# Another list of batches: optional work placed elsewhere between the scores of an attention kernel

## The chip, the cores and the metric

The kernel runs on one core of a Trainium2 chip. The metric is the device time of one execution in microseconds; three runs of the kernel before gave 647.3, 646.79 and 646.97, median 646.97. The core's engines are TensorE (PE in the profile, with its weight loads as PEld), VectorE (DVE), ScalarE (ACT), GpSimd (POOL) and SyncE (SP), which here only issues transfers. All of them run their own instruction streams in order and wait for each other on semaphores.

## The reference, cut to what matters

Two independent results are computed from two inputs of 2048 rows by 448 columns and put side by side.

```python
q = heads(x @ wq)              # 16 heads of 28 columns
k = x @ wk; v = x @ wv         # one key and one value head, shared by all 16
p = softmax(q k^T * 28**-0.5)  # 16 x 2048 x 2048
a = concat(p v) @ wo

X = rfft2(x2); X = X * (w_r + 1j * w_i); b = irfft2(X)
```

The attention part dominates: 16 heads times 2048 queries times 2048 keys of exponentials. The spectral filter (a transform over columns and rows, a product, and the way back) is much smaller and is cut into pieces that are slipped in between.

## The kernel before

**Projections.** The first 69 us of the profile form queries, keys and values, and the first pieces of the filter's forward transform. The change leaves them alone, except for one piece that it moves (below, F).

**Steps.** What follows is 256 steps: 4 blocks of 512 queries, times 4 groups of 4 heads, times 16 blocks of 128 keys. A step has four scores, one for each head: a matmul (line 867, `s<-qa,ka`, 128 keys by 512 queries) that fills one PSUM bank. ScalarE makes the exponential of a bank into SBUF (line 811, `p<-s`), and then the bank is free again. The output phase multiplies the exponentials with the values (line 822, `s<-p,vs`; eight records for a step) and sums 16 steps into one bank. After the 16th step VectorE transposes that bank out (line 826) and a new group of 4 heads begins. The group needs its own query tile `qa`, made by `build_q`: three VectorE instructions (lines 217, 219, 208), eight small transfers (line 213) and, once those have landed, one transfer of 512 KB (line 215), all issued by SP. `build_q` is put into VectorE's list after the fourth step of the group before. In this document q4 and q5 are the query tiles of steps 64 and 80.

**Banks.** There are eight PSUM banks: six named `s`, and `sx` and `po`. One of them holds the output being summed. So seven are left for scores and for the optional units below; each is taken by `take()` and handed back by `give()`, which decide at build time, by a rough clock of their own, which bank is taken next.

**Batches.** The list PLAN has 50 strings; one string is one batch. Of each batch all scores are formed first, then the outputs. In a string `-` is a score whose exponential ScalarE makes from the bank; `k` is a score of the batch's last step that VectorE copies out of its bank (line 873, `k<-s`), so that ScalarE can make the exponentials of that step later, two wide instructions (line 890); `e` is a score of the last step whose exponential ScalarE writes at once. The last step's outputs are formed in the next batch. Since its four `k` scores stand among the first eight, a batch whose last step opens a new group needs that group's `qa` from its second score on. Batches of five steps have 20 scores ("fives"), batches of six have 24 ("sixes").

**Units.** The other letters are pieces of other work, each with its own bank:

- F, once: the last piece of the filter's first stage (line 159), read out by VectorE and stored for the second stage.
- A, 16 times (lines 556 to 558, three matmuls): second stage; VectorE then reads the bank three times (601 to 603) and goes on for five more instructions (609 to 611, 587, 588).
- B, 16 times (lines 556 to 558 too, with `g2`): the stage after; VectorE copies the bank out (625), and after every second B the tile is stored by SP (629).
- W, 48 times, in fours (line 731, 11 matmuls): the output projection of one block of 128 rows; one bank for four, read by VectorE (738).
- Z, 32 times, in twos: the last stage, in turn two transforms (line 655, read by line 658) and two more (line 669, read by lines 673 to 675). In the text z stands for a pair of the first kind and y for a pair of the second.

VectorE also normalises each finished group (lines 703, 708, 722, 723, 718), with 8 KB transfers behind it (line 692 on SP, 695 on GpSimd). VectorE, ScalarE and TensorE run in the order in which the program writes them. Between the letters the function `passed` lets waiting VectorE work go in by the rough clock; so another string also changes VectorE's order. The transfers of SP and GpSimd are ordered by the scheduler.

`spread(n, units, lazy, start, rest)` writes a string: it sets unit number j behind about 4(n-1)·(j+start)/(units+rest) scores. A larger start sets the units later; a smaller rest spreads them wider.

Of the kernel before, what the change touches and what calls it, by code (L numbers as in the profile page):

```python
# [37 lines left out]
def spread(n, units, lazy=4, start=0.9, rest=0.85):  # L38

    m = 4 * n - 4  # L40
    out = [(float(i), "-") for i in range(m)]
    out += [(j + 0.5 if j < lazy else m + 0.1 * j, "k" if j < lazy else "e") for j in range(4)]
    out += [(m * (j + start) / (len(units) + rest) - 0.4, u) for j, u in enumerate(units)]
    return "".join(k for _, k in sorted(out)).replace("X", "WWWW").replace("Y", "ZZ")


PLAN = ["eeeeF", "eeee"] + 4 * [spread(2, "", 0)]
FIVE, SIX = spread(5, "BA"), {u: spread(6, u) for u in ("X", "Y", "BAX", "XBB")}
PLAN += [spread(5, "A", 4, 1.6), spread(5, "A")] + 11 * [FIVE] + [SIX["X"], FIVE, SIX["X"], SIX["BAX"], FIVE]
PLAN += [SIX["XBB"], spread(5, "")]  # L50
PLAN += 4 * [SIX["Y"]] + 4 * [SIX["X"]] + 7 * [SIX["Y"]] + 4 * [SIX["X"]] + 3 * [SIX["Y"]] + 2 * [spread(5, "Y")]


WARM = 10, 10
# [3 lines left out]
def kernel(ctx: ExitStack, tc: tile.TileContext, t: dict):  # L58
# [713 lines left out]
    where, total = {}, 0  # L772
    for tokens in PLAN:
        n, x = sum(k in "-ke" for k in tokens) // 4, 0
# [71 lines left out]
    begin = 0  # L846
    for tokens in PLAN:
        n = sum(k in "-ke" for k in tokens) // 4
# [273 lines left out]
```

## Time and profile before

| | before |
|---|---|
| median of three runs | 646.97 us |
| the profiled execution | 646.39 us |
| its span, first to last instruction | 644.5 us |
| TensorE busy | 639.0 us |
| ScalarE busy | 552.6 us |
| VectorE busy | 370.6 us |
| mean granted TensorE clock | 0.999 |

The profiled execution lies 0.58 us under the median, and its time is 1.9 us more than its span. Matmuls overlap in the records, so TensorE looks busy even where the next matmul starts late; a wait shows in the distance between starts rather than as idle time. The view of stretches, asked for from one batch's first score to the next one's, gives a batch's length and each engine's busy time in it. In the timeline view equal instructions that follow each other are merged into one row with a count.

### The profile page before, as it was taken

Reading aid. Unit: us, or ns where it says so; the run is one execution under the profiler, and the core shown is the slowest. Engines: PE = TensorE matmul, PEld = TensorE weight load, DVE = VectorE, ACT = ScalarE, POOL = GpSimd, SP = SyncE. Lnnn points to the kernel's source line nnn. Section 1 sums busy time; section 2 is a strip of 40 time slices with the busy share of each in tenths; the row PEclk is TensorE's granted clock in tenths of the full one; section 3 lists DMA queues with packets and bytes.
Section 4 is the critical chain, followed back from the end, with each engine's and each line's share of the span. In section 5 each row is a group of like instructions: output and inputs, shape, how many; then the busy total and the mean of one; then the engine's idle time right before and its main releaser. Section 6 shows DMA issues by size and latency. Waiting matters only on the chain.

```text
span 644.5 us, 12021 instructions
## 1 busy us (share of the span) xinstructions
PE 639.0 (99%) x4470; PEld 381.5 (59%) x4470; DVE 370.6 (58%) x683; ACT 552.6 (86%) x1011; POOL 79.9 (12%) x150
## 2 busy tenths in 40 slices
PE   9999999999999999999999999999999999999997
PEld 7877555555555556655555566556655566556655
DVE  5999538989997937465543523354545342363531
ACT  5655999999998989988999898998999898998891
POOL 3022301001211110001020300011031100010110
PEclk9999999999999999999999999999999999999999
DMA  8766953446734522213242403014241403131001
GB/s 275 263 182 167 269 135 101 115 99 155 189 87 112 142 59 72 55 59 103 56 114 59 114 16 80 29 41 122 52 122 42 103 15 80 44 92 20 30 31 60
DMA packets 36113, 63.83 MB, mean 99 GB/s; under 512 B 7905, under 2 KB 23922, under 8 KB 35084
## 3 DMA queue, kind: packets, MB, share of 16 engines
q1 hardware_dynamic: 30832, 49.60, 27.7%
q0 software_dynamic: 4640, 12.48, 7.5%
q10 hardware_dynamic: 576, 0.92, 0.4%
q8 instruction: 36, 0.59, 0.4%
q14 instruction: 29, 0.24, 0.1%
HBM read 30.04 MB, written 14.75 MB: 69 GB/s over the span
## 4 chain that ended last, share of the span: by engine, by line
PE 96%; DMA 1%; DVE 1%; SPq 1%; issue 0%; ACT 0%; ACTq 0%; DVEq 0%
PE s L867 30%; PE s L822 23%; PE po L822 7%; PE s L342 6%; PE sx L867 5%; PE sx L822 4%; PE po L867 4%; PE s L731 4%; PE s L140 2%; PE s L655 2%; PE s L669 2%; PE po L731 1%; PE pbb L159 1%; DMA qa<-qa 1%; PE s L290 1%; PE s L558 1%
## 5 line engine op out<-in xcount | busy, mean ns | idle before, releaser
L811 ACT ACTIVATE p<-s 128x512 f32<-128x512 f32 x632 | 340.1, 627 | 37.1 <-PE s L867 31.4
L867 PE MATMUL s<-qa,ka 128*128 128x512 f32 x782 | 238.0, 407 | 0.3 <-DMA qa<-qa 0.2
L867 PEld LDWEIGHTS s<-qa,ka 128*128 128x128 f32 x782 | 143.2, 188 | 73.7 <-issue 33.1
L873 DVE COPY k<-s 128x512 f32<-128x512 f32 x131 | 84.1, 683 | 125.4 <-PE s L867 125.4
L822 PE MATMUL s<-p,vs 128*32 128x512 f32 x1112 | 132.3, 595 | 0.0
L890 ACT ACTIVATE k<-k 128x1024 f32<-128x1024 f32 x88 | 90.3, 1108 | 0.0
L822 PEld LDWEIGHTS s<-p,vs 128*32 128x32 f32 x1112 | 33.5, 109 | 72.6 <-issue 70.9
L811 ACT ACTIVATE p<-sx 128x512 f32<-128x512 f32 x109 | 68.3, 626 | 7.0 <-PE sx L867 6.4
L811 ACT ACTIVATE p<-po 128x512 f32<-128x512 f32 x83 | 52.8, 636 | 4.8 <-PE po L867 2.3
L867 PE MATMUL sx<-qa,ka 128*128 128x512 f32 x130 | 53.2, 409 | 0.0
L867 PE MATMUL po<-qa,ka 128*128 128x512 f32 x112 | 45.2, 403 | 0.0
L822 PE MATMUL s<-k,vs 128*32 128x512 f32 x296 | 38.7, 594 | 0.0
L822 PE MATMUL po<-p,vs 128*32 128x512 f32 x328 | 38.5, 594 | 0.0
L695 POOL DMA_DIRECT2D ol<-ol x36 | 18.0, 508 | 130.1 <-DVE ol L718 65.4
L679 POOL TENSOR_TENSOR yo<-y 128x226 f32<-128x226 f32 x16 | 9.5, 596 | 190.7 <-DVE y L675 98.1
L867 PEld LDWEIGHTS sx<-qa,ka 128*128 128x128 f32 x130 | 24.4, 188 | 12.7 <-issue 5.0
L873 DVE COPY k<-po 128x512 f32<-128x512 f32 x27 | 18.5, 683 | 16.4 <-PE po L867 16.2
L867 PEld LDWEIGHTS po<-qa,ka 128*128 128x128 f32 x112 | 21.1, 188 | 7.6 <-issue 2.5
L822 PE MATMUL sx<-p,vs 128*32 128x512 f32 x208 | 24.8, 595 | 0.0
L826 DVE STREAM_TRANSPOSE osb<-s 128x512 f32<-128x512 f32 x11 | 7.9, 716 | 29.2 <-PE s L822 29.2
L822 PEld LDWEIGHTS po<-p,vs 128*32 128x32 f32 x328 | 9.8, 110 | 21.9 <-issue 21.3
L342 PE MATMUL s<-xh,wqh 128*128 128x512 f32 x56 | 22.7, 404 | 0.0
(224 smaller groups left out, 780.6 us busy)
## 6 DMA issues: line engine op xcount, KB each, us to landing
qa<-qa SPq DMA_DIRECT2D x15, 512.0 KB
raw<-xa SPq DMA_DIRECT2D x16, 256.0 KB
xb<-xb SPq DMA_DIRECT2D x8, 512.0 KB
qa<-qh SPq DMA_DIRECT2D x64, 64.0 KB
qa<-ql SPq DMA_DIRECT2D x60, 64.0 KB
ob<-yo SPq DMA_DIRECT2D x16, 226.0 KB
t<-bs SPq DMA_DIRECT2D x16, 225.0 KB
wr<-wr POOLq DMA_DIRECT2D x16, 225.0 KB, 4.6
```

The source lines that it names most:

```text
L140: mm(pa[r0:r0 + 32, e, o0:o0 + n], f[:, 2 * r + k, 2 * p + e, h], cs1[:, 2 * r + k, :n], start=True, stop=True)
L342: mm(pq, w[:, j, gs], x[:, j], start=(j == 0 and n == 0), stop=(j == 3 and n == 1))
L655: mm(pz[:w, j], c2["c", q][:, j, o0:o0 + w], c2["F", q][:, j], start=True, stop=True)
L669: mm(py[:, k], z[:w, r, js], cs3[:w, k], start=True, stop=True)
L679: nc.gpsimd.tensor_tensor(yo[:, 0:2], y1[:, 0], y1[:, 1], op=ALU.add)
L695: nc.gpsimd.dma_start(ol[c][o, g].bitcast(F32), ol[c][r, 0].bitcast(F32))
L731: mm(p, x[c][:, g, s], w, start=(g == 0 and n == 0), stop=(g == NG - 1 and n == 2))
L811: nc.scalar.activation(tiles[-1][:, h % 2], sc, AF.Exp, scale=SCALE)
L822: mm(po[c, g][32 * i:32 * i + 32], vs[:, kc], ps[i // 2][:, i % 2], start=(n == 1), stop=(n == 16))
L867: begun.append(mm(sc, ka[:, kc * 128:(kc + 1) * 128], qa[c, g][:, h], start=True, stop=True))
L873: nc.vector.tensor_copy(keep[h // 2][:, h % 2], sc)
L890: nc.scalar.activation(p, p, AF.Exp, scale=SCALE)
```

## The change

Only PLAN changes. The numbers of batches (50), of fives and sixes, of scores of each kind and of units of each kind stay the same.

```diff
-PLAN = ["eeeeF", "eeee"] + 4 * [spread(2, "", 0)]
-FIVE, SIX = spread(5, "BA"), {u: spread(6, u) for u in ("X", "Y", "BAX", "XBB")}
-PLAN += [spread(5, "A", 4, 1.6), spread(5, "A")] + 11 * [FIVE] + [SIX["X"], FIVE, SIX["X"], SIX["BAX"], FIVE]
-PLAN += [SIX["XBB"], spread(5, "")]
-PLAN += 4 * [SIX["Y"]] + 4 * [SIX["X"]] + 7 * [SIX["Y"]] + 4 * [SIX["X"]] + 3 * [SIX["Y"]] + 2 * [spread(5, "Y")]
+PLAN = ["eeee"] + ["eeeeF"] + [spread(2, "", 0, 1.05)] + 3 * [spread(2, "", 0)] + [spread(5, "A", 4, 1.6)]
+PLAN += [spread(5, "BA", 4, 0.9, 0.6)] + [spread(5, "A")] + 6 * [spread(5, "BA", 4, 0.9, 0.6)]
+PLAN += [spread(5, "BA", 4, 0.75, 0.6)] + 3 * [spread(5, "BA", 4, 0.9, 0.6)] + 2 * [spread(6, "X")]
+PLAN += [spread(5, "BA", 4, 0.9, 0.6)] + [spread(6, "BAX")] + [spread(5, "BAB", 4, 0.9, 0.6)]
+PLAN += [spread(6, "BX")] + [spread(6, "Y")] + [spread(5, "")] + 2 * [spread(6, "Y")]
+PLAN += [spread(6, "Y", 4, 0.9, 0.6)] + [spread(6, "X")] + [spread(6, "X", 4, 0.9, 0.6)] + [spread(6, "X")]
+PLAN += [spread(6, "Y")] + [spread(6, "X", 4, 0.9, 0.6)] + 3 * [spread(6, "Y")]
+PLAN += [spread(6, "Y", 4, 0.9, 0.73)] + [spread(6, "Y")] + [spread(6, "Y", 4, 0.9, 0.73)]
+PLAN += 3 * [spread(6, "X")] + [spread(6, "Y")] + [spread(6, "X", 4, 0.9, 0.73)] + [spread(5, "Y")]
+PLAN += [spread(6, "Y")] + [spread(6, "Y", 4, 1.2)] + [spread(5, "Y")]
```

Written out, the batches whose string changes (counted from 0; the rest is the same):

```
batch   before                        after
0, 1    eeeeF / eeee                  eeee / eeeeF
7       -k-k-k-k----A--------         -k-k-k-k--B------A----
8       -k-k-k-k-B------A-----        -k-k-k-k----A--------
9-14    -k-k-k-k-B------A-----        -k-k-k-k--B------A----
15      -k-k-k-k-B------A-----        the same
16-18   -k-k-k-k-B------A-----        -k-k-k-k--B------A----
20      -k-k-k-k-B------A-----        -k-k-k-k------WWWW----------
21      -k-k-k-k------WWWW----------  -k-k-k-k--B------A----
23      -k-k-k-k-B------A-----        -k-k-k-kB-----A----B---
24      -k-k-k-k-WWWW-----B-----B-----  -k-k-k-k--B-------WWWW-------
25      -k-k-k-k------------          -k-k-k-k------ZZ----------
26      -k-k-k-k------ZZ----------    -k-k-k-k------------
29      -k-k-k-k------ZZ----------    -k-k-k-k-------ZZ---------
31      -k-k-k-k------WWWW----------  -k-k-k-k-------WWWW---------
33      -k-k-k-k------WWWW----------  -k-k-k-k------ZZ----------
34      -k-k-k-k------ZZ----------    -k-k-k-k-------WWWW---------
38, 40  -k-k-k-k------ZZ----------    -k-k-k-k-------ZZ---------
44      -k-k-k-k------WWWW----------  -k-k-k-k------ZZ----------
45      -k-k-k-k------ZZ----------    -k-k-k-k-------WWWW---------
46      -k-k-k-k------ZZ----------    -k-k-k-k----ZZ--------
48      -k-k-k-k----ZZ--------        -k-k-k-k---------ZZ-------
```

VectorE's and SP's orders follow. In batch 17, for one, the three instructions of `build_q` for q5 stood behind everything that follows A; after the change they stand right behind the three that read A's bank (603), ahead of 609 to 611, 587 and 588. In SP's list the 512 KB transfer of the query tile of step 32 comes behind a store of B's tile (629) instead of ahead of it.

## The prediction

> **What bounds the kernel.** I read the page first, then the batches as stretches, then the last scores of two batches in the timeline.
>
> ```profile
> PE 639.0 (99%) x4470; PEld 381.5 (59%) x4470; DVE 370.6 (58%) x683; ACT 552.6 (86%) x1011; POOL 79.9 (12%) x150
> PE 96%; DMA 1%; DVE 1%; SPq 1%; issue 0%; ACT 0%; ACTq 0%; DVEq 0%
> ```
>
> TensorE carries the chain, and its matmuls are the same before and after. So the change can only alter how long TensorE waits. The page hides those waits in 639.0 us of "busy"; the lengths of batches show them (columns: stretch; length; busy PE, PEld, DVE, ACT, POOL; clock; DMA share; GB/s).
>
> ```profile
> 163.41:174.11 10.70, 10.70 (x71) 5.92 (x67) 10.02 (x19) 9.92 (x18) 4.78 (x9) 1.00 0.73 197
> 206.59:217.08 10.49, 10.49 (x70) 6.00 (x66) 9.74 (x18) 9.80 (x18) 2.05 (x4) 1.00 0.32 99
> 99.33:109.85 10.52, 10.52 (x68) 5.44 (x64) 8.49 (x15) 9.87 (x19) 3.16 (x6) 1.00 0.31 80
> ```
>
> These are batches 13 and 17 (both with B and A) and 7 (A alone). 13 and 17 do the same matmuls; 13 takes 0.21 us longer. Their ends:
>
> ```profile
> 168.94 0.81 PE L867 MATMUL s<-qa,ka 128*128 128x512 f32 x2
> 169.25 0.49 PE L867 MATMUL s<-qa,ka 128*128 128x512 f32 x1
> 169.68 0.64 PE L822 MATMUL s<-p,vs 128*32 128x512 f32 x4
> 212.34 0.39 PE L867 MATMUL s<-qa,ka 128*128 128x512 f32 x1
> 212.66 1.06 PE L822 MATMUL s<-p,vs 128*32 128x512 f32 x8
> ```
>
> Unhindered scores start 0.23 us apart. In batch 13 the last of 20 starts 0.31 us after the one before (168.94 is the merged row of the last two, 169.25 the last), and the outputs start 0.43 us later, against 0.32 in batch 17 (212.34, 212.66): a late last score costs its wait and then 0.11 at the change to outputs. Outputs begin 6.27 us into batch 13, 6.07 into batch 17. The last score waits for a bank. With seven banks for 22 takes the last needs the 15th release: four copies, B's copy, and ten exponentials. In batch 17 the group before has just ended and left an eighth bank, so nine do. ScalarE's rows:
>
> ```profile
> 164.00 3.73 ACT L811 ACTIVATE p<-s 128x512 f32<-128x512 f32 x7 [0.70 <-PE s L867]
> 167.62 0.60 ACT L811 ACTIVATE p<-sx 128x512 f32<-128x512 f32 x1
> 170.00 0.67 ACT L811 ACTIVATE p<-po 128x512 f32<-128x512 f32 x1
> 170.48 0.68 ACT L811 ACTIVATE p<-sx 128x512 f32<-128x512 f32 x1
> ```
>
> An exponential starts every 0.48 to 0.49 us (170.00, 170.48), yet the eighth starts 3.62 us after the first: 7 x 0.49 = 3.43, so 0.19 was lost. That is the hole that B tears: it stands after nine scores, five of them for ScalarE, which runs dry while B's matmuls run.
>
> **The change, part by part.** Durations from the profiled execution.
>
> *Units one score later in fives (9 to 14, 16, 18).* B after ten scores gives ScalarE a sixth score, 0.49 us of work, more than the hole. Without it the tenth exponential ends at 0.59 + 0.60 + 9 x 0.49 = 5.60 us into the batch; the last score's own place is 5.75 (212.34 - 206.59). No wait: 10.49 for 10.70. Eight batches: -1.7. Batch 8 becomes like 7: -0.2; 7 keeps 10.5. Batch 15 stays. Together -1.9. What hides the moved B and A is the seven banks of stored scores. The price is on VectorE: A's list starts 0.2 later in a batch 0.2 shorter, and VectorE is busy 10.02 of 10.70. Its copies (873) then come late, with the banks they free. Bounds: -2.1 to +0.5.
>
> *q5 earlier in VectorE's list.* Batch 19 against 21 (its string before the change is the same):
>
> ```profile
> 227.80:241.94 14.14, 13.94 (x88) 7.94 (x84) 3.11 (x5) 12.14 (x22) 1.98 (x4) 1.00 0.12 38
> 252.45:265.88 13.43, 13.43 (x87) 7.93 (x83) 3.85 (x7) 12.11 (x23) 0.00 (x0) 1.00 0.39 95
> 213.54 0.69 DVE L609 SCALAR_TENSOR_TENSOR pwr<-pwi,sgn,pwr 128x450 f32<-128x450 f32 x1
> 216.21 0.54 DVE L217 TENSOR_SCALAR ql<-qraw,mask,cvec 128x512 f32<-128x512 f32 x1
> 217.28 0.54 SPq L213 DMA_DIRECT2D qa<-qh  x1
> 224.01 0.51 SPq L215 DMA_DIRECT2D qa<-qa  x1
> 228.50 0.47 PE L867 MATMUL s<-qa,ka 128*128 128x512 f32 x1 [0.20 <-DMA qa<-qa]
> ```
>
> From 217.28 to 228.50 q5 needs 11.2 us: eight issues, a landing, the large transfer. Five VectorE instructions (609 to 588, from 213.54 to 216.21, 2.7 us) now go behind it. It comes 2.7 us sooner where 0.7 us was missing: -0.7 (bounds -0.7 and 0). What they delay, B of batch 18 and A of 18, is a batch away.
>
> *q4, batch 16.* Nothing moves it:
>
> ```profile
> 195.53:206.59 11.06, 10.96 (x70) 6.00 (x67) 7.84 (x14) 10.06 (x18) 2.34 (x5) 1.00 0.55 144
> 188.65 0.34 SPq L629 DMA_DIRECT2D t<-cst  x1
> 189.71 0.62 SPq L692 DMA_DIRECT2D oh<-ol  x1
> 190.55 0.52 SPq L215 DMA_DIRECT2D qa<-qa  x1
> ```
>
> Its large transfer is queued on SP behind B's store and a small transfer that wait for VectorE in batch 15; every late VectorE there is paid by TensorE in full. Batch 16 loses some 0.4 us now. I add +0.3 (bounds 0 and +1, about a k copy and B's).
>
> *20 and 21 swapped.* Batch 20 has the eighth bank too, and gives it to W, whose late last score it spares: 10.49 (as 17) + 13.43 becomes 13.32 + 10.49: -0.1.
>
> *23 and 24.* B leaves 24, and W goes later.
>
> ```profile
> 291.33:306.47 15.14, 15.14 (x94) 9.05 (x90) 9.52 (x17) 12.00 (x22) 2.10 (x5) 1.00 0.36 101
> 280.62:291.33 10.71, 10.71 (x71) 6.01 (x67) 8.05 (x15) 9.92 (x18) 0.00 (x0) 1.00 0.26 81
> 165.61 0.37 PE L556 MATMUL po<-ph,g2h 128*128 128x450 f32 x1
> 166.22 0.62 PE L867 MATMUL s<-qa,ka 128*128 128x512 f32 x2
> ```
>
> B costs 0.61 us of TensorE (165.61 to 166.22). After: 10.49 + 0.61 = 11.10, and a W six without its last wait, 13.32, + 0.61 = 13.93; 25.03 for 25.85: -0.8 (bounds -0.85 and -0.3, if 23's last score, which takes A's bank, waits for VectorE). The last B, after ten of 24 scores, is now copied some 13 us ahead of the first z, which reads what it stores: 11 us of batch 24 behind it and 3 of 25 less a copy. Before, that path begins so:
>
> ```profile
> 300.53 0.33 SPq L629 DMA_DIRECT2D t<-cst  x1
> 303.74 0.58 POOL L646 DMA_DIRECT2D c<-t  x1 [53.98 <-DMA oh<-ol]
> ```
>
> 3.2 us for the store until the first load is issued, and the q5 rows bound a landing by 4.5: under 8 of 13.
>
> *25 and 26, 33 and 34, 44 and 45.* z and y pairs next to VectorE's query or normalising work cost more:
>
> ```profile
> 316.50:329.67 13.17, 13.17 (x92) 7.53 (x89) 8.01 (x15) 12.38 (x23) 2.54 (x5) 1.00 0.23 60
> 342.60:355.48 12.88, 12.88 (x92) 7.60 (x88) 5.44 (x9) 11.95 (x22) 0.00 (x0) 1.00 0.14 38
> 422.43:435.55 13.12, 13.12 (x92) 7.54 (x88) 8.02 (x15) 12.00 (x22) 2.55 (x5) 1.00 0.23 56
> 567.56:580.73 13.17, 13.17 (x92) 7.55 (x88) 8.14 (x17) 11.98 (x22) 3.03 (x5) 1.00 0.46 117
> 368.65:382.08 13.43, 13.43 (x87) 7.91 (x83) 3.11 (x5) 12.00 (x22) 0.00 (x0) 1.00 0.13 42
> 374.73 0.60 ACT L811 ACTIVATE p<-s 128x512 f32<-128x512 f32 x1 [0.48 <-PE s L867]
> 376.36 0.50 PE L867 MATMUL s<-qa,ka 128*128 128x512 f32 x1
> 376.79 0.64 PE L822 MATMUL s<-p,vs 128*32 128x512 f32 x4
> ```
>
> Batches 26, 34 and 45 stand at 13.17, 13.12 and 13.17 beside 12.88 (28) where VectorE is free. After the swap W, whose matmuls outlast ScalarE's stock (0.48 idle in batch 30, 13.43 long), stands beside that work, and z or y where VectorE is free. 26 to 25: -0.3. 33/34: 13.43 + 13.12 to 12.88 + 13.31: -0.35; 44/45: 13.43 + 13.17 to 12.95 (y, whose readers are three; estimated between 28 and 34) + 13.31: -0.35. 13.31 is W one score later: ScalarE's hole shrinks, the last score is no longer late, and the 0.11 at the change to outputs (376.36, 376.79: 0.43) goes; the same in 31: -0.1. Units one score later in 29, 38 and 40 spare the same 0.11, or half of it where it is half paid, and a little of ScalarE's hole: -0.15, -0.05, -0.15; 46 to 48 (the five's pair away from the normalising), for which I have no row of its kind: -0.1. Together -1.55; bounds -1.8 and -0.6.
>
> *F* moves from between scores to ahead of outputs and saves one return to scores, where the second starts 0.1 late: -0.1 (bounds -0.3 and 0). Its readers, VectorE's copies, have half a microsecond until `sx` and `po` are wanted in batch 2.
>
> Sum: -1.9 - 0.7 + 0.3 - 0.1 - 0.8 - 1.55 - 0.1 = -4.85. 646.39 - 4.85 = 641.5 for an execution like the profiled one; the median lies 0.58 higher: 642.1.
>
> The sum rests on interleaving: stretches in which ScalarE or VectorE is short next to such in which TensorE is. [...]
>
> **Rivals.**
>
> *ScalarE is the bound.* Its 9.92 us in batch 13 and the 0.70 it idles at each start make 10.62, and a later B shifts but does not shorten that. Fives then fall by 0.08 only, -0.7 for -1.9: 643.3. Against it: 17 runs in 10.49 with the same 0.70 idle:
>
> ```profile
> 207.19 1.09 ACT L811 ACTIVATE p<-s 128x512 f32<-128x512 f32 x2 [0.70 <-PE s L867]
> ```
>
> [...]
>
> *VectorE becomes the bound in 9 to 15.* At 10.02 of a wanted 10.49 it runs behind, its copies free banks late, the fives stay at 10.7 and q4 slips by a further 0.7: -4.85 + 1.9 + 0.7 = -2.25: 644.7.
>
> *Slower: a query tile behind a B store.* The tile of step 32 now has its large transfer behind the store of batch 9's B. q4's was issued 5.0 us ahead of its batch (190.55, 195.53) and was late; a tile that waits for B's store of the batch before has about as long. If the tiles of steps 32 to 80 and the later ones each slip so, every microsecond is TensorE's; above 0.4 us for each of twelve tiles the gain is gone. At 0.6: 646.97 - 4.85 + 7.2 = 649.3. For it: batches 16 and 19 show such waits. Against: those two stand out by their length, the others quoted don't.
>
> *No change:* the rough clock that hands out banks may undo the order, so that fives and swaps give back what q5 wins: 646 to 647.
>
> **How the numbers follow.** This kernel's runs can tell about 0.2%, 1.3 us, from no change. The sum as forecast 0.62; ScalarE 0.13; VectorE 0.13; tiles late 0.06; no change 0.06. Predicted 642.1; its own range is 641 to 643.2 (bounds of fives and swaps). The range 640.8 to 645.2 takes in the first three. Faster 0.88, within 0.06, slower 0.06.
>
> **What would show it.** Right: batches 9 to 14 and 18 of 10.5 us, with ScalarE's hole gone; 19 at 13.4 with no wait for `qa`; 23 and 24 together 25.0; 45 and 34 at 13.3. Wrong: VectorE's first copy more than 1 us into a five; a wait for `qa<-qa` at a batch's start other than 16; fives at 10.6 or more with no bank wait left.

## The result and the profile after

| | before | after |
|---|---|---|
| median of six runs each | 647.01 us | 642.50 us |
| all runs | 646.79 to 647.43 | 641.86 to 642.98 |
| the profiled execution; its span | 646.39; 644.5 | 642.82; 641.0 |
| first score of the main loop in the span | 69.00 | 70.45 |
| the loop: from there to the end of the last batch's outputs | 560.85 | 555.93 |

The ratio is 0.9928, with an interval of 0.9915 to 0.9941. The forecast was 642.1 us. The loop, on which the forecast's sum was made, is 4.92 us shorter (the sum said 4.85). The start-up of the profiled execution is 1.45 us longer, and the span therefore only 3.5 us shorter; more on this below. (The expectations below let the loop end 12.00 us later, among the matmuls behind the last batch: 567.9 there is 555.93 here. What they call the start of the last batch is the end of its outputs.)

The page of the changed kernel, first TensorE's and the other engines' busy time, then the chain that ended last:

```profile
PE 635.7 (99%) x4470; PEld 381.8 (60%) x4470; DVE 372.3 (58%) x683; ACT 550.7 (86%) x1011; POOL 80.1 (12%) x150
...
PE 98%; DMA 1%; ACT 0%; SPq 0%; issue 0%; ACTq 0%
```

Nothing in these lines tells where the time went. The stretches from one batch's first score to the next one's do (columns as in the prediction). Here are batches 13, 14, 16, 19, 23, 24 and 34 of the changed kernel (45 takes 13.31, as 34):

```profile
163.79:174.32 10.53, 10.53 (x71) 6.00 (x67) 10.06 (x19) 9.83 (x18) 4.29 (x8) 1.00 0.94 218
174.32:184.95 10.63, 10.63 (x71) 5.93 (x67) 10.27 (x20) 9.89 (x18) 0.00 (x0) 1.00 0.48 112
195.65:206.16 10.51, 10.51 (x71) 6.03 (x67) 7.93 (x14) 9.82 (x18) 2.34 (x5) 1.00 0.60 152
227.18:240.71 13.53, 13.53 (x87) 7.94 (x83) 3.22 (x6) 12.05 (x22) 2.00 (x4) 1.00 0.10 31
279.29:290.64 11.35, 11.35 (x73) 6.53 (x69) 8.58 (x16) 9.92 (x18) 0.00 (x0) 1.00 0.22 69
290.64:304.57 13.93, 13.93 (x90) 8.51 (x86) 9.11 (x16) 12.01 (x22) 1.14 (x2) 1.00 0.49 138
419.42:432.73 13.31, 13.31 (x87) 7.92 (x83) 10.13 (x19) 12.00 (x22) 0.47 (x1) 1.00 0.27 70
```

Batch 13, 10.70 us before, takes 10.53. Its end, in TensorE's timeline, and ScalarE's timeline in the same batch:

```profile
168.86 1.10 PE L872 MATMUL s<-qa,ka 128*128 128x512 f32 x4
169.89 1.06 PE L827 MATMUL sx<-p,vs 128*32 128x512 f32 x8
```

```profile
164.39 0.60 ACT L816 ACTIVATE p<-po 128x512 f32<-128x512 f32 x1 [0.70 <-PE po L872]
164.88 4.52 ACT L816 ACTIVATE p<-s 128x512 f32<-128x512 f32 x9
169.26 0.63 ACT L816 ACTIVATE p<-po 128x512 f32<-128x512 f32 x1
```

The last four scores and the change to the outputs take 1.03 us (168.86 to 169.89), which is three steps of 0.235 and one of 0.325: none is late. On ScalarE eleven exponentials start from 164.39 to 169.26, one every 0.487 us; the hole of 0.19 us in the middle of the batch has gone.

Summed by the parts of the forecast, from the lengths of all batches:

| part | forecast | measured in the two profiles |
|---|---|---|
| fives 7 to 16 and 18 | -1.9 | -1.6 (16 against its length without a wait for q4, 10.72) |
| q4, batch 16 | +0.3 | -0.3 (11.06 had a wait for q4, 10.51 has none) |
| q5, batch 19 | -0.7 | -0.6 (14.14 to 13.53) |
| 20 and 21 | -0.1 | -0.1 |
| 23 and 24 | -0.8 | -0.55 (25.84 to 25.29) |
| 25 to 48, placing of z, y and W | -1.55 | -1.6 (0.2 of it in 37 and 43, which no term names) |
| F | -0.1 | -0.1 |

### The profile page after: what moved, and what is told of

It is laid out like the page before. It is cut to its first block, busy times and chain, and to the rows that moved or that the text cites. A ratio compares the mean times of both kernels' runs of the same rounds, so it can differ in the third digit from the quotient of the medians.

```text
span 641.0 us, 12024 instructions
## 1 busy us (share of the span) xinstructions
PE 635.7 (99%) x4470; PEld 381.8 (60%) x4470; DVE 372.3 (58%) x683; ACT 550.7 (86%) x1011; POOL 80.1 (12%) x150
## 4 chain that ended last, share of the span: by engine, by line
PE 98%; DMA 1%; ACT 0%; SPq 0%; issue 0%; ACTq 0%
PE s L872 31%; PE s L827 22%; PE sx L827 9%; PE s L347 6%; PE po L872 5%; PE po L827 4%; PE s L736 4%; PE sx L872 4%; PE s L145 2%; PE s L674 2%; PE s L660 2%; PE pbb L164 1%; DMA raw<-wq 1%; PE s L562 1%; PE s L561 1%; PE s L563 1%
## 5 line engine op out<-in xcount | busy, mean ns | idle before, releaser
L816 ACT ACTIVATE p<-s 128x512 f32<-128x512 f32 x650 | 345.9, 631 | 33.4 <-PE s L872 27.5
L827 PE MATMUL s<-p,vs 128*32 128x512 f32 x1024 | 121.7, 595 | 0.0
L816 ACT ACTIVATE p<-sx 128x512 f32<-128x512 f32 x85 | 53.6, 630 | 3.1 <-PE sx L872 1.9
L827 PE MATMUL sx<-p,vs 128*32 128x512 f32 x416 | 49.3, 594 | 0.0
L872 PE MATMUL po<-qa,ka 128*128 128x512 f32 x120 | 49.2, 410 | 0.0
L872 PE MATMUL sx<-qa,ka 128*128 128x512 f32 x106 | 42.4, 400 | 0.0
L827 PE MATMUL s<-k,vs 128*32 128x512 f32 x256 | 33.4, 594 | 0.0
L827 PEld LDWEIGHTS sx<-p,vs 128*32 128x32 f32 x416 | 12.5, 110 | 27.9 <-issue 27.6
L827 PE MATMUL po<-p,vs 128*32 128x512 f32 x208 | 25.0, 595 | 0.0
L872 PEld LDWEIGHTS sx<-qa,ka 128*128 128x128 f32 x106 | 19.9, 188 | 6.7 <-issue 2.5
```

Of the source, the lines that this page charges most:

```text
L816: nc.scalar.activation(tiles[-1][:, h % 2], sc, AF.Exp, scale=SCALE)
L827: mm(po[c, g][32 * i:32 * i + 32], vs[:, kc], ps[i // 2][:, i % 2], start=(n == 1), stop=(n == 16))
L872: begun.append(mm(sc, ka[:, kc * 128:(kc + 1) * 128], qa[c, g][:, h], start=True, stop=True))
```

## The experiments

All experiments change strings of PLAN unless it is said otherwise, and all of them compute everything. The theory is the prediction's: a unit must not come so early that ScalarE runs out of stored scores while it lasts. Since batches depend little on one another but for the query tiles, one kernel can try several things in different batches.

**The fives alone** (`b_fives`: before, with batches 7 to 14, 16 and 18 as after).

```diff
-9-14, 16, 18  -k-k-k-k-B------A-----
+9-14, 16, 18  -k-k-k-k--B------A----
 17            -k-k-k-k-B------A-----
```

> The kernel before with the strings of batches 7 to 14, 16 and 18 alone taken from the changed kernel; 17 stays as before. Theory (a hole in ScalarE's work after nine scores makes the last score late): batches 9 to 14 and 18 of 10.51 to 10.53 us where before has 10.70 to 10.72, 14 perhaps 10.63 as in the changed kernel; 16 between 10.5 and 10.8, as its large query transfer happens to land; 19 stays at 14.1, since the instructions of batch 17 are not moved in VectorE's list; everything from 20 on as before. The loop is 1.6 to 2.1 us shorter than before's, the time 645.2 for 647.0. Rival (VectorE's order or an earlier start-up gave the gain): fives at 10.7. Start-up: if the 1.45 us by which the changed kernel's first score came later (69.00 before, 70.45 after) is chance, this kernel's lies anywhere between these; if it comes from the list of batches, it is 69.0 here, since F stands as before.

Batches 13, 16 and 19 of this kernel:

```profile
163.55:174.07 10.52, 10.52 (x70) 6.00 (x66) 9.97 (x19) 9.81 (x18) 4.27 (x8) 1.00 0.93 219
195.43:205.94 10.51, 10.51 (x70) 6.00 (x66) 7.93 (x14) 9.82 (x18) 2.32 (x5) 1.00 0.58 152
226.97:241.06 14.09, 13.67 (x88) 7.94 (x84) 3.22 (x6) 12.14 (x22) 2.00 (x4) 1.00 0.12 39
```

The other fives with a new string take 10.51 to 10.53 and 14 takes 10.64, as in the changed kernel, and 19 still waits for q5. The loop is 558.84 us, 2.0 less than before's, of which 0.34 is a wait of 16 that is not here (nor in a second profile of before, below). The time is 645.51 us beside 647.09 (ratio 0.9975, 0.9966 to 0.9984). The first score stands at 70.12, although F is where it was: the late start-up does not need the new head of the list.

**Where the unit stands** (`dose1`).

```diff
-9, 10, 11  -k-k-k-k--B------A----
+9          -k-k-k-k-B-------A----
+10         -k-k-k-k--B-----A-----
+11         -k-k-k-kB--------A----
-12, 13, 14 -k-k-k-k--B------A----
+12         -k-k-k-k----B----A----
+13         -k-k-k-k--B--A--------
+14         -k-k-k-k-B------A-----
-21         -k-k-k-k--B------A----
+21         -k-k-k-Bk--------A----
```

> The changed kernel (units after 10 and 16 scores, 10.51) with other places in single batches. Theory: only the scores ahead of B count, because ScalarE's stock of 0.49 us each must last over B. Batch 9, B after 9 and A after 16: 10.70. Batch 10, B 10 and A 15: 10.51. Batch 11, B after 8: a hole of about 0.48 for 0.22, so about 11.0. Batch 12, B after 12 and A after 16: 10.51, no further gain, since TensorE itself is then the bound. Batch 13, B 10 and A 12: 10.5. Batch 14, B 9 and A 15 as before: 10.70. Batch 21, B after 7 (the next score is a copied one, so that the hole is as with 8): 11.0. Rival (A's place counts): 9 at 10.5 and 10 at 10.7. Rival (ScalarE's total is the bound): 12 under 10.45 or all alike. Rival (VectorE is the bound): 12 and 13 above 10.6, as B's copy comes late.

The seven batches in that order:

```profile
121.15:131.86 10.71, 10.71 (x70) 6.01 (x66) 8.66 (x16) 9.92 (x18) 2.09 (x4) 1.00 0.54 144
131.86:142.38 10.52, 10.52 (x71) 6.02 (x67) 9.27 (x18) 9.82 (x18) 0.56 (x1) 1.00 0.46 105
142.38:153.35 10.97, 10.97 (x70) 5.92 (x66) 10.55 (x19) 9.92 (x18) 0.00 (x0) 1.00 0.29 86
153.35:163.88 10.53, 10.53 (x70) 6.01 (x66) 9.68 (x18) 9.82 (x18) 4.79 (x9) 1.00 0.58 135
163.88:174.42 10.54, 10.54 (x70) 6.02 (x66) 9.79 (x18) 9.84 (x18) 1.26 (x3) 1.00 0.77 192
174.42:185.16 10.74, 10.74 (x70) 5.93 (x66) 10.28 (x20) 9.92 (x18) 1.90 (x4) 1.00 0.48 132
254.27:265.25 10.98, 10.98 (x71) 6.00 (x67) 7.54 (x13) 9.92 (x18) 0.59 (x1) 1.00 0.47 120
```

B after 9 scores costs 0.2 us (0.1 in 14, which takes 10.63 otherwise), after 8 or 7 0.46 us, after 10 or 12 nothing; A's place does not matter. All three rivals fall: A's place, ScalarE's total and, in these batches, VectorE.

**q5, F and the four W of 24 set back** (`a_back`).

```diff
-0, 1  eeee / eeeeF
+0, 1  eeeeF / eeee
-17    -k-k-k-k--B------A----
+17    -k-k-k-k-B------A-----
-24    -k-k-k-k--B-------WWWW-------
+24    -k-k-k-k-WWWW-----B----------
```

> The changed kernel with four batches set back: F again in batch 0, batch 17 as before, and in batch 24 the four W after nine scores as before, but with one B only. Theory: the first row of batches 0.11 longer (4.19 for 4.08); batch 17 stays at 10.50 (eighth bank), but 19 goes from 13.53 to 14.1, because q5's instructions in VectorE's list again stand behind 609 to 588; 24 goes from 13.94 to about 14.5 (before's 15.14 less 0.61 for the B that left). Rival for 19 (q5 came earlier because batches 8 to 16 keep VectorE less behind): 19 stays at 13.5. Rival for 24 (the second B was the whole cost): 13.9.

Batches 17, 19 and 24:

```profile
206.39:216.88 10.49, 10.49 (x71) 6.00 (x67) 9.75 (x18) 9.81 (x18) 2.06 (x4) 1.00 0.33 100
227.40:241.47 14.07, 13.65 (x87) 7.94 (x83) 3.24 (x6) 12.14 (x22) 2.00 (x4) 1.00 0.12 39
291.39:306.04 14.65, 14.65 (x90) 8.48 (x86) 9.11 (x16) 12.00 (x22) 2.54 (x5) 1.00 0.49 133
```

F's return costs its 0.11 (4.19 us). The string of batch 17, which does not shorten 17, shortens 19. So q5's place in VectorE's list is the cause; `b_fives`, with the old batch 17, agrees. In 24 the B that left took 0.5 us with it (15.14 to 14.65), and the new places of W and of the B that stayed the other 0.7. `dose1`, `a_back`, `a_swaps`, `before_again`, `dose2`, `after_again` and `a_zapart` were run once each; what is read from them is the length of batches.

**The exchanges undone** (`a_swaps`: 20/21, 25/26 and 33/34 as before; of 44/45 only the exchange).

```diff
-44, 45  -k-k-k-k------ZZ---------- / -k-k-k-k-------WWWW---------
+44, 45  -k-k-k-k-------WWWW--------- / -k-k-k-k------ZZ----------
```

> The changed kernel with the exchanges undone: 20/21, 25/26 and 33/34 as before; 44/45 exchanged back, but W kept one score later. Theory (z and y lose next to VectorE's own work, W does not): 20+21 23.93 for 23.84; 25+26 23.2 for 22.90; 33+34 26.55 for 26.19; 44+45 13.31 + 13.17 = 26.48 for 26.32, half of that pair's gain from the later W and half from the exchange. Rival (all the gain of such a pair is W's later place): 44+45 stays at 26.3.

The sums are 23.93, 23.20, 26.57 and 26.49 us. The last pair:

```profile
551.19:564.51 13.32, 13.32 (x87) 7.93 (x83) 7.48 (x14) 12.00 (x22) 0.00 (x0) 1.00 0.05 18
564.51:577.68 13.17, 13.17 (x93) 7.57 (x89) 8.13 (x17) 11.98 (x22) 3.03 (x5) 1.00 0.48 119
```

So W's later place is worth 0.11 (13.43 to 13.32) and the exchange 0.17; the rival is half right.

**Before once more** (`before_again`, the kernel before unchanged).

> The kernel before once more, for a second profiled execution. If the short start-up of the first one (first score 69.00 us into the span; 69.9 to 70.6 in the five other profiles so far, whichever list they run) was chance, this one starts at 69.6 or later, and its time is about 647.0 to 647.6; if it comes from the list, 69.0 again. Batch 16: if the large transfer for q4 lands late whenever batches 9 to 14 are of 10.7 us, it is 11.06 again (all five other profiles with shorter fives have 10.5 to 10.6); if the wait was chance, 10.72. All other batches as in the first profile within 0.05.

Batch 16 takes 10.72 us, without a wait: the one of the first profile does not belong to the program. Measured from this profile, the change makes the loop 4.7 us shorter. All other batches agree within 0.04, apart from 19 (14.23 for 14.14). The first score stands at 68.94, which by the expectation speaks for the list of batches as the reason of the early start, and the time is 646.04.

**W and Z at other places** (`dose2`).

```diff
-30, 32, 41, 42, 43  -k-k-k-k------WWWW----------
+30                  -k-k-k-k----WWWW------------
+32                  -k-k-k-k--------WWWW--------
+41                  -k-k-k-k-------WWWW---------
+42                  -k-k-k-k---------WWWW-------
+43                  -k-k-k-k--WWWW--------------
-27, 28, 35, 36, 39, 47  -k-k-k-k------ZZ----------
+27, 35              -k-k-k-k-------ZZ---------
+28, 39              -k-k-k-k--------ZZ--------
+36                  -k-k-k-k----ZZ------------
+47                  -k-k-k-k--ZZ--------------
```

> The changed kernel with W and Z after other numbers of scores in single batches of six steps. Theory (ScalarE's stock must last over W's 2.2 us): W after 10 scores (batch 43) about 14.4, after 12 (30) about 13.95, after 14 (the value now) 13.43, after 15 (41) 13.31, after 16 (32) 13.3, after 17 (42) 13.3 to 13.5, since seven banks do not hold the scores that run ahead. Z after 10 (47, y) and 12 (36, z) is shorter work, so 13.2 and 12.95 at most; after 15 (27: 12.9, 35: 12.95) and 16 (28: 12.82, 39: 12.95). Rival (the last score is late for VectorE's sake and not ScalarE's): W's length does not depend on its place, 13.3 to 13.4 throughout.

Batches 30 (W after 12 scores), 36 (Z after 12), 41, 42 and 43 (W after 15, 17 and 10); 32 (W after 16) takes 13.30 and 39 (Z after 16) 13.27:

```profile
365.29:379.24 13.95, 13.95 (x87) 7.94 (x84) 3.11 (x5) 12.00 (x22) 0.00 (x0) 1.00 0.12 41
445.11:458.50 13.39, 13.39 (x92) 7.61 (x88) 5.44 (x9) 12.00 (x22) 0.00 (x0) 1.00 0.13 36
510.79:524.10 13.31, 13.31 (x87) 7.92 (x84) 3.75 (x6) 12.00 (x22) 0.00 (x0) 1.00 0.05 18
524.10:537.63 13.53, 13.53 (x87) 7.85 (x84) 4.76 (x9) 11.90 (x22) 0.00 (x0) 1.00 0.34 85
537.63:552.09 14.46, 14.46 (x88) 7.95 (x84) 3.11 (x5) 12.00 (x22) 0.00 (x0) 1.00 0.09 27
```

W follows the theory to 0.06 us. Z does not: earlier it loses 0.5 us (36) and, after 10 scores, 1.0 (47: 13.98), where at most 0.2 was expected, and later it loses 0.1 to 0.3 in 27, 35 and 39 and nothing in 28. The expectation seems to have had Z too short. In the changed kernel's TensorE timeline a y pair holds up the next score for 1.70 us:

```profile
330.84 1.94 PE L674 MATMUL s<-cs,z 113*128 113x113 f32 x16
332.54 0.94 PE L872 MATMUL s<-qa,ka 128*128 128x512 f32 x3
```

With that length one rule covers B, Z and W; it is an estimate from the rows above. After n scores ScalarE has n - 4 exponentials (four scores are VectorE's) that start 0.49 us apart, the first 0.60 us into the batch (163.79 to 164.39 in batch 13); the last takes 0.60, so it runs dry at about 0.70 + 0.49 (n - 4). The score behind a unit of length L starts at 0.10 + 0.23 n + L (0.10 is what the second score of a batch is late: in batch 13 it starts 0.34 us behind the first for the usual 0.23), and its exponential 0.6 later. So 0.26 n must reach 1.95 + L: n of about 10 for B (0.61: 166.23 to 166.84 in the changed kernel's batch 13), 14 for a pair of Z (1.7), 16 for W (2.23: 423.02 to 425.25 in batch 34).

**A version further by that rule** (`v1`: W after 15 or 16 scores; 15 like its neighbours; the units of 22 one score later; the two Z apart; a Z in 26; B in batch 8 instead of at the end of 23).

```diff
-8, 23  -k-k-k-k----A-------- / -k-k-k-kB-----A----B---
+8, 23  -k-k-k-k--B------A---- / -k-k-k-k--B------A----
-25, 26 -k-k-k-k------ZZ---------- / -k-k-k-k------------
+25, 26 -k-k-k-k------Z---------- / -k-k-k-k----Z--------
-28     -k-k-k-k------ZZ----------
+28     -k-k-k-k----Z---Z---------
...
```

> The changed kernel, taken further by the same rule: a unit of length L stands where ScalarE's stock lasts over it, after n scores with 0.26 n >= 1.95 + L us (B 0.61: 10; Z pair 1.67: 14; one Z 0.84: 11; W 2.23: 16), and no later, as its bank must come back in time. W after 15 or 16 in 19, 30, 32, 41 to 43: 13.31 for 13.43 each, -0.7. Batch 15 like its neighbours: 10.52, -0.2. Batch 22 B, A and W one score later each: 14.53, -0.2. Z pairs taken apart in 27 to 48, the two Z some three to five scores from each other: 12.75 where a pair takes 12.88 to 13.00, 12.9 to 13.0 where it takes 13.07 to 13.16: -1.9 in all. One Z of batch 25 into the empty batch 26, which ScalarE bounds: 22.2 for 22.90, -0.7. B also in batch 8, which ScalarE bounds (10.51), and so none at the end of 23: 8 stays at 10.51 and 23 goes from 11.35 to 10.51, -0.84. Together -4.5: a loop of 563.4 us for 567.9, and 638.0 us for 642.5. Rival for batch 8 (VectorE is the bound of the early fives; it would be busy 10.36 us of 10.51): its copies come late, 8 and the fives behind it take 10.6 to 10.8, and 16 and 19 wait for their query tiles. Rival for the Z apart (VectorE's reading, not ScalarE's stock, sets the length): 12.9 to 13.1 as before. Rival (W's bank or the scores ahead): W batches at 13.4.

Measured were 642.25 us (ratio 0.9925, 0.9911 to 0.9938): no better than the changed kernel. The loop is shorter by 1.1 us, not 4.5. Batches 8, 16 and 25 (23 takes 10.52):

```profile
110.19:120.70 10.51, 10.51 (x70) 6.01 (x66) 10.15 (x19) 9.82 (x18) 0.00 (x0) 1.00 0.79 204
194.34:205.70 11.36, 10.78 (x70) 6.01 (x67) 7.65 (x14) 10.02 (x18) 0.00 (x0) 1.00 0.58 163
303.10:315.94 12.84, 12.84 (x84) 6.66 (x80) 4.68 (x8) 11.89 (x22) 2.04 (x4) 1.00 0.16 43
```

W, 8, 15 and 23 came as expected; VectorE, busy 10.15 of batch 8's 10.51 us, held nothing up. Three things did not, and 22 (14.80 for 14.53) and 29 (13.37, longer than the 13.07 of the pair) did not either; why was not looked into.

First, batch 25 with one Z instead of two (84 instructions of TensorE for 92) still takes 12.84 us. Its last scores still wait for banks that ScalarE frees: ScalarE is busy 11.89 us of the 12.84. So taking two Z apart can bring 13.00 down to 12.86 but 12.88 no further than 12.84. Here the rival "ScalarE is the bound" holds.

Second, what batch 23 won, 16 lost: its second score waits for q4. TensorE's and SP's timelines of `v1`:

```profile
194.35 0.50 PE L872 MATMUL s<-qa,ka 128*128 128x512 f32 x1
195.43 0.47 PE L872 MATMUL po<-qa,ka 128*128 128x512 f32 x1 [0.58 <-DMA qa<-qa]
```

```profile
188.85 1.89 SPq L697 DMA_DIRECT2D oh<-ol  x3
190.93 0.52 SPq L220 DMA_DIRECT2D qa<-qa  x1
```

Third, the end of the program takes 1.15 us longer (below).

**The changed kernel once more, and v1 mended** (`after_again`; `v2`: v1 with 22, 25, 26, 29, 36, 38, 39 and 46 as after, 37's pair after 15, and one line changed).

> The changed kernel once more, for a second profiled execution. If the start-up (first score 70.45 us into the span in the first one; 68.94 in the second one of before, 69.3 in two others with the new list, 70.1 in one that starts like before) is chance, it is anywhere from 68.9 to 70.5; if it comes from the list, 70.4 again. Batches as in the first profile within 0.05, apart from 19, which is 13.42 to 13.53 as the transfer for q5 lands, and 16, 10.5 to 10.6.

All batches agree within 0.02, apart from 19 (13.65). The first score stands at 70.06, the time is 642.61.

```diff
-            nc.sync.dma_start(oh[c][o, g].bitcast(F32), ol[c][r, 0].bitcast(F32))
+            nc.gpsimd.dma_start(oh[c][o, g].bitcast(F32), ol[c][r, 0].bitcast(F32))
```

> v1 with what fell there set back (22, 25, 26, 29, 36, 38, 39 and 46 as in the changed kernel; 37 a pair one score later), and the 8 KB transfers of line 697 issued by GpSimd instead of SP. Theory for batch 16 of v1 (11.35 us, the second score 0.85 late): the 512 KB transfer for q4 stands on SP behind three of these small ones, which wait for VectorE's line 723, and is issued 3.4 us ahead of its batch for 5.0 in the changed kernel. Without them on SP it is issued up to 2.5 us sooner and 16 takes 10.52. Rival (the transfer is slow in itself, or its eight small ones land late): 16 stays above 10.8. The rest as in v1: 23 10.52, W batches 13.31, 8 and 15 10.52. Together 2.6 us less than the changed kernel's loop: 565.3, and 639.9 us.

Batch 16 is back at 10.52 us: it was the place in SP's queue. The loop is 553.54 (565.5 as the expectation counts it), but the time is 642.55 (641.04 to 643.21; ratio 0.9928, 0.9913 to 0.9942) for the 639.9 expected. The end is as late as in v1, and the runs are spread wider.

**The end of the program** (`v3`: v2 with the Z of 27, 28 and 33 together; `a_zapart`: the changed kernel with the Z of 27, 28, 33, 35, 44 and 47 apart).

> v2 with the Z of batches 27, 28 and 33 together again, so that ScalarE's stream has 269 instructions of its sequencer (waits and branches) as before has, for 276 in v2. Theory for the end of v1 and v2 (between ScalarE's two sequencer steps at line 940 lie 2.5 us, in the eight other profiles 0.41): it depends on the length of ScalarE's stream, and the way past it falls between 269 (before) and 276 (v2). Then 0.41 us here, and the span is again 14.7 us longer than the start of the last batch, for 15.8 in v2. The loop is 565.6 to 565.8 (v2 565.57, plus 0.15 for the three batches). Time 640.4 to 641.0 with a start-up like the others' (69.5 to 70.3). Rival (the end is late because GpSimd has SP's small transfers, or because of the W and B places): 2.5 us again, 641.6 to 642.5.

> The changed kernel with only the two Z of batches 27, 28, 33, 35, 44 and 47 taken apart as in v1: ScalarE's stream has 279 sequencer instructions for 265. Theory (length of ScalarE's stream): 2.5 us between the two steps at line 940 and the end 1.15 us later, though the loop is 0.5 us shorter (35 and 44 12.86 for 13.0, 27 12.86, 28 and 33 12.84, 47 12.93), so the time is 0.6 us above the changed kernel's at an equal start-up. Rival: 0.41 us, and 0.5 us less.

Behind the last store the program branches past a block that is not run. ScalarE's sequencer at that line (start of the first and the last), in `v3` and in `a_zapart`:

```profile
L940 ACTq COMPARE_BRANCH  x1: 54/54/54, 637.8 to 637.8; - x1
L940 ACTq EVENT_SEMAPHORE  x1: 17/17/17, 638.3 to 638.3; - x1
```

```profile
L940 ACTq COMPARE_BRANCH  x1: 54/54/54, 638.0 to 638.0; - x1
L940 ACTq EVENT_SEMAPHORE  x1: 17/17/17, 640.6 to 640.6; - x1
```

0.41 us and 2.5 us lie between them; the span's end comes 1.15 us later for it, since what follows the second step takes 0.97 us there for 1.90. All eleven profiles with 1272 to 1280 records on ScalarE have 0.41 there, the three with 1287 (v2), 1290 (a_zapart) and 1300 (v1) have 2.5. Z apart gives ScalarE more waits, each an instruction of its own: 1290 records in `a_zapart` for 1276 in the changed kernel. The view of transfers between the two steps, `a_zapart` and then `v3`:

```profile
q14 instruction: 1, 0.01, 1.2%
```

```profile
q10 hardware_dynamic: 105, 0.19, 104.6%
```

The second shows stores of the result alone. The first, which stands beside such stores, is a load of instructions, 8 KB, which starts 0.95 us behind the branch. `v1` and `v2` have such a load between the steps, the eleven others have none. `a_zapart`, run once, has a loop 0.4 us shorter than the changed kernel's and takes 643.31 us.

`v3` took 642.1 us (641.4 to 644.04; ratio 0.9929, 0.9916 to 0.9943) for the 640.4 to 641.0 expected, and shows one way in which the runs of v2 and v3 can be spread. GpSimd issues eight small transfers in a row now, and W of batch 19 waits for one of them, in TensorE's timeline:

```profile
233.77 0.47 PE L736 MATMUL sx<-wox,ol 128*128 128x448 f32 x1 [1.66 <-DMA ol<-ol]
```

Batch 19 takes 15.29 us there, and the loop 1.9 more than in v2. In v2 the same eight are issued in the same places; there they land within 1.9 us and batch 19 takes 13.62, while in v3 one takes 3.4 us. So the late landing is not fixed by the list; whether it would happen with four of them on SP was not tried. At the end the 0.41 us are back.

**Only what touches no queue** (`v4`: the changed kernel with W later in 19, 30, 32 and 41 to 43, Z apart in 35, 44 and 48, 37's pair after 15).

> The changed kernel with W after 15 or 16 scores in 19, 30, 32 and 41 to 43, the two Z of 35, 44 and 48 apart, those of 37 after 15; nothing that moves VectorE's or SP's order around the query tiles q4 and q5, and fewer sequencer instructions on ScalarE than before. Theory: W batches 13.31 for 13.43 (-0.6), 19 -0.1, 35 and 44 12.86 for 13.00 (-0.3), 37 13.07 and 48 12.98 (-0.2): a loop of 566.7 us for 567.9, 0.41 us at line 940, no wait for a query tile of more than 0.3 us, and 641.3 us for 642.5. Rival (what v1 to v3 won was lost again to start-up and landing transfers whatever the list): 642.0 or more, with batch 16 or 19 above 10.8 or 13.7.

Batch 35 (30 takes 13.31):

```profile
432.08:444.94 12.86, 12.86 (x93) 7.67 (x89) 4.65 (x10) 11.90 (x22) 4.83 (x10) 1.00 0.45 120
```

641.42 us (641.08 to 641.71) beside 646.91, ratio 0.9914 (0.9901 to 0.9928). It has the lowest median of these kernels, 1.1 us under the changed one, but the two were not timed side by side and the intervals of their ratios overlap; their loops differ by 1.3 us in the profiles.

## Why the prediction was right

The forecast, 642.1 us, lies 0.4 under the measured median, and it was right for the reason given: most of what changed is TensorE's waits for banks that ScalarE frees late. `dose1` shows the mechanism by itself, and `b_fives`, `a_back` and `a_swaps` show three of its terms alone. That the sum meets the loop to 0.1 us is partly luck: q4's term was wrong by 0.6 one way, the fives, q5, 23 and 24 together by 0.6 the other way.

- *Fives.* 10.51 to 10.53 for the forecast 10.49, in seven batches with B. Batch 14 is the exception, 10.63. There VectorE transposes and divides a finished group first, and its first copy starts 1.41 us into the batch (175.73 - 174.32):

```profile
174.08 0.71 DVE L831 STREAM_TRANSPOSE osb<-sx 128x512 f32<-128x512 f32 x1
...
175.12 0.69 DVE L713 TENSOR_TENSOR osb<-osb,r 128x512 f32<-128x512 f32 x1
175.73 2.48 DVE L878 COPY k<-s 128x512 f32<-128x512 f32 x4
```

  That is the sign which the prediction named for VectorE as the bound; B starts 0.1 us late. So that rival holds for one batch, by 0.1 us.
- *q4.* The step that failed: a single wait of the first profile was read as a property of the program, and VectorE's later A was added to it. `before_again` has no such wait, and all profiles with shorter fives but v1's have 10.5 to 10.62 in batch 16; in the changed kernel the transfer is issued 5.0 us ahead of the batch, as in before, and nothing waits. What is true of the step is how close it is: `v1`, where it is issued 3.4 us ahead, pays 0.84.
- *q5.* -0.6 for -0.7; the rest lies in how the transfer lands (13.42 to 13.65 in six profiles in which only q5's place counts). `a_back` shows that it is the order in VectorE's list.
- *20/21, 25 to 48, F.* Within 0.1 of their terms, pair by pair (44/45 brought 0.28 for 0.35). 46 to 48, for which no row existed, brought nothing instead of 0.1. What the terms of 25 to 48 miss is made up by 37 (13.25 to 13.16) and 43 (13.56 to 13.43), whose strings did not change; the prediction does not name them, and why they became shorter was not looked into.
- *23 and 24.* -0.55 for -0.8, inside the bounds. The term that was too large is 23, 11.35 for 11.10: its last score is late by 0.16 us and pays the 0.1 at the change to the outputs. The prediction named a wait of that score for VectorE, which frees A's bank, as its bound, and the trace has it, on the score's weight load (608 is VectorE's last reading of A's bank):

```profile
285.79 0.19 PEld L872 LDWEIGHTS s<-qa,ka 128*128 128x128 f32 x1 [0.21 <-DVE pwr L608]
```

  24 came out at 13.94, as forecast.
- *ScalarE as the bound.* It fell for the fives: they take 10.52 and not 10.62, and batch 26, a five with the same exponentials but no unit, takes 10.02. What ScalarE does set is when the last score gets its bank. Batch 8, with A alone and so 0.6 us less work for TensorE, takes 10.51 like its neighbours; its last three scores wait for ScalarE, the last of them here:

```profile
116.84 0.19 PEld L872 LDWEIGHTS s<-qa,ka 128*128 128x128 f32 x1 [0.31 <-ACT p L816]
```

  Its outputs start 6.09 us into the batch, those of 13 6.10. So with B in its best place TensorE's own work and ScalarE's frees end together, which is why `v1` could put a B into batch 8 for nothing and why B after 12 scores brings no more than after 10. The rival holds for sixes with Z. ScalarE's 86% is a mean over stretches which it bounds (sixes with Z: 12.84 us in `v1`'s batch 25 with one Z, 12.88 with two in the changed kernel) and others which it does not (the fives: 10.52 us, and not 10.62).
- *The tiles behind a B store.* In the two profiles of the changed kernel only batch 19 waits for a query tile, by 0.02 and 0.13 us. That rival falls here, though `v1` shows the danger on the same queue.
- *The way to the median.* The prediction carried the loop's gain over to the median in full (0.58 us is what the median of before lies above its profile). The loop came out 4.92 us shorter and the median 4.51: the 0.4 us by which the forecast is off lie, as far as the profiles show, in the start-up.

The start-up stays partly open. First scores stand at 69.00 and 68.94 in the two profiles of before and at 69.28 to 70.57 in the twelve of other lists. It goes with the first loads: ScalarE's waits for `wq` in the first 12 us, in before and in after:

```profile
ACT wqh L322 <- DMA raw<-wq: 3.2, 3, 1.7
```

```profile
ACT wqh L327 <- DMA raw<-wq: 5.6, 4, 2.5
```

`b_fives` (70.12) begins with the same strings as before and `dose2` (69.28) with those of after, so the head of the list does not decide it. The timed runs of before reach from 646.28 to 647.84 with both profiles at the lower end, which speaks for chance; that both profiles of before agree at 69.0 speaks against it. Whether a few tenths depend on the program was not settled.

## What to carry to other kernels

A piece of TensorE work put between matmuls that feed another engine had a best place here, worked out from three durations (0.23 us a score, 0.49 an exponential, and the piece's own): not before the other engine's stored work lasts over it (B after 9 scores costs 0.2 us, after 10 nothing), and not so late that the end is held up (13.53 us with W after 17 scores, 13.30 after 16; that its bank or the stored scores are short by then is an estimate). The gain came from one late instruction at the end of each stretch (10.70 to 10.53 us in batch 13), so it must be read from the length of equal stretches and not from busy time. When a list is retuned, look at every queue that it reorders: what a place won here (0.84 us in batch 23) a transfer behind three others lost in another batch.

## What the runs showed of the hardware that was not expected

Where the strings agree, batch lengths agree within 0.05 us in all fourteen profiles, apart from 14, 16, 19, 29, 37 and 43 (0.1 to 2 us), so that one profiled execution tells 0.1 us. Whole runs of one kernel differ by 0.5 to 2.6 us; where two profiles of one kernel differ, it is in the start-up and in single transfers.

The step behind the branch at the end comes 0.41 us after it in the eleven profiles with 1272 to 1280 recorded instructions on ScalarE and 2.5 us after it in the three with 1287 to 1300, and only in these three does a load of 8 KB of instructions lie between the two. That the step waits for this load, and that a longer program is what puts the load there, would fit; it was not shown, as no row names the load as what ScalarE waits for.
